# Attention feeding a gated feed-forward layer: q, k and v loaded per head pair and cast on chip, both heads' scores in one two-bank tile, one shared PSUM pool, and the weights loaded behind the third pair

## The chip, the cores and the metric

The kernel runs on one core of one Trainium2 chip. The metric is device time in microseconds (us), the median of several executions. All executions quoted here are of the fast state; the executions of one kernel lie between 0.1% and 1.1% apart (1.1% in e9). A ratio is the mean time of one kernel's fast runs over the mean of the other's of the same rounds, so it is not quite the ratio of the medians quoted.

The names of the engines: PE is TensorE's matmul stream, PEld its weight loads, DVE is VectorE, ACT is ScalarE, POOL is GpSimd, SP is SyncE, which only issues transfers here. "L203" is a line of the kernel's source. In the kernel with the change, and in every variant, POOL's lines are: L166 and L167 cast q and k, L173 scales v, L203 is the causal mask, L283 is `rs`, the last step of the norm. (Line numbers move by a few in some variants; the names say what it is.)

## The reference

```python
# q, k, v: (8 batches, 8 heads, 576, 64) fp32; f: (8, 8, 576), in 0.8 .. 1.0
cum    = cumsum(log(clip(f, 1e-4, 1)))
scores = q @ k^T / 8 + (cum_i - cum_j), masked above the diagonal
attn   = softmax(scores)
x      = (attn @ v), heads joined: 4608 rows of 512
# feed-forward, d_ff = 1536
xn  = x / rms(x) * rms_g
out = (silu(xn @ w_gate) * (xn @ w_val)) @ w_out
```

Both kernels fold the decay into v: exp of the plain scores is masked, and v, with a column of ones beside it, is multiplied by `exp(mid - cum_j)`. The same matmul then gives numerator and denominator.

## The kernel before

Batch 0's attention runs alone; this is the prologue. Then nine groups of 512 rows go through the feed-forward, and the attention of batches 1 to 7 is woven between their matmuls. `LEAD = 6` puts some attention work of batch 1, called the lead below, ahead of the first gate in program order. The last groups have no attention beside them; they are the tail.

The loads. q and k come with a cast to bf16 in the transfer, issued by POOL, a whole batch at a time; v comes from SP in fp32 and is scaled by POOL.

```python
def load_qk(b):
    for j in range(NB):
        p0, n = j * 128, min(128, S - j * 128)
        for src, dst in ((q, qb[b % 2]), (k, kb[b % 2])):
            nc.gpsimd.dma_start(
                out=dst[0:n, j, :].rearrange("p (h d) -> p h d", d=D),
                in_=src[b, :, p0:p0 + n, :].rearrange("h p d -> p h d"))
# ... (cut)
load_qk(0); load_v(0)
# ... (cut: constants)
for i in range(3):
    load_w(i)          # POOL: 512 columns of w_gate and of w_val each
load_qk(1); load_v(1)
load_wo()              # POOL: w_out in two transfers
for _, work in attention(0):
    work()
```

PSUM, the memory that matmuls write, is used as eight banks of 512 fp32 columns. Scores have three tiles of one bank, the feed-forward three, transposes and values one each.

```python
ps_tr = ctx.enter_context(tc.tile_pool(name="ps_tr", bufs=1, space=PSUM))
ps_sc = ctx.enter_context(tc.tile_pool(name="ps_sc", bufs=3, space=PSUM))
ps_o = ctx.enter_context(tc.tile_pool(name="ps_o", bufs=1, space=PSUM))
ps_f = ctx.enter_context(tc.tile_pool(name="ps_f", bufs=3, space=PSUM))
```

Scores go head by head; a head pair's two heads lie in the two halves of the 128 rows.

```python
def scores(b, p, bank):
    for par in range(2):
        # ... (cut)
        rows = slice(par * 64, par * 64 + 64)
        sc = ps_sc.tile([128, 512], F32, name="sc")
        for kj, q0, n, c in BANKS[bank]:
            nc.tensor.matmul(sc[:, c:c + n], lhsT=KT[b, p][rows, kj * 128:(kj + 1) * 128],
                             rhs=QT[b, p][rows, q0:q0 + n], start=True, stop=True)
        t = PT[b, h]
        nc.scalar.activation(t[:, bank * 512:(bank + 1) * 512], sc, ACT.Exp, scale=scale)
        # ... (cut: masks on POOL for banks 0 and 2)
```

The gate uses two tiles of its own:

```python
def gate(g, fc):
    pg = ps_f.tile([128, GT], F32, name="ff")
    # ... four matmuls with wg into pg
    nc.scalar.activation(t, pg, ACT.Tanh, scale=0.5)
    nc.vector.scalar_tensor_tensor(a, in0=t, scalar=1.0, in1=pg, op0=ALU.add, op1=ALU.mult)
    pv = ps_f.tile([128, GT], F32, name="ff")
    # ... four matmuls with wv into pv
    nc.vector.scalar_tensor_tensor(hTs[g][:, fc, :], in0=a, scalar=0.5, in1=pv, op0=ALU.mult, op1=ALU.mult)
```

The softmax here doesn't subtract the row's maximum and nothing guards it: scores larger than these inputs give would overflow.

Of the kernel before, what the change touches and what calls it, by code (L numbers as in the profile page):

```python
# [23 lines left out]
def kernel(  # L24
# [12 lines left out]
    nc = tc.nc  # L37
# [11 lines left out]

    consts = ctx.enter_context(tc.tile_pool(name="consts", bufs=1))  # L50
    ldp = ctx.enter_context(tc.tile_pool(name="ldp", bufs=1))
    vp = ctx.enter_context(tc.tile_pool(name="vp", bufs=6))
    qkt = ctx.enter_context(tc.tile_pool(name="qkt", bufs=2))
    ptp = ctx.enter_context(tc.tile_pool(name="ptp", bufs=5))
# [4 lines left out]
    hp = ctx.enter_context(tc.tile_pool(name="hp", bufs=2))  # L59
    ep = ctx.enter_context(tc.tile_pool(name="ep", bufs=3))  # L60
    ps_tr = ctx.enter_context(tc.tile_pool(name="ps_tr", bufs=1, space=PSUM))
    ps_sc = ctx.enter_context(tc.tile_pool(name="ps_sc", bufs=3, space=PSUM))
    ps_o = ctx.enter_context(tc.tile_pool(name="ps_o", bufs=1, space=PSUM))
    ps_f = ctx.enter_context(tc.tile_pool(name="ps_f", bufs=3, space=PSUM))


    qb = [ldp.tile([128, NB, H * D], BF16, name=f"qb{i}") for i in range(2)]
    kb = [ldp.tile([128, NB, H * D], BF16, name=f"kb{i}") for i in range(2)]
    Vs = [ldp.tile([128, NB, H, D + 1], BF16, name=f"Vs{i}") for i in range(2)]
    PT4 = [[ldp.tile([128, 5 * 64], BF16, name=f"PT4_{i}{j}") for j in range(2)] for i in range(2)]  # L70


    def load_qk(b):
        for j in range(NB):
            p0, n = j * 128, min(128, S - j * 128)
            for src, dst in ((q, qb[b % 2]), (k, kb[b % 2])):
                nc.gpsimd.dma_start(  # L77
                    out=dst[0:n, j, :].rearrange("p (h d) -> p h d", d=D),
                    in_=src[b, :, p0:p0 + n, :].rearrange("h p d -> p h d"))

    v32s = {}

    def load_v(b):
        for j in range(NB):
            p0, n = j * 128, min(128, S - j * 128)
            v32 = v32s[b, j] = vp.tile([128, H, D], F32, name="v32")
            nc.sync.dma_start(out=v32[0:n, :, :],
                              in_=v[b, :, p0:p0 + n, :].rearrange("h p d -> p h d"))

    fr = consts.tile([BH, S], F32)  # L90
    nc.sync.dma_start(out=fr, in_=f.rearrange("b h s -> (b h) s"))

    for t in qb + kb:
        nc.vector.memset(t[64:128, NB - 1, :], 0.0)
    load_qk(0)
    load_v(0)
    for t in Vs:
        nc.vector.memset(t[64:128, NB - 1, :, :], 0.0)
    for pair in PT4:
        for t in pair:  # L100
            nc.vector.memset(t[:, 4 * 64:], 0.0)
# [5 lines left out]

    rg = consts.tile([128, NDC], F32)
    with nc.allow_non_contiguous_dma(reason="512 gains, once"):
        nc.sync.dma_start(out=rg, in_=moe_rms_g.rearrange("(c p) -> p c", p=128))  # L110
    mhalf = consts.tile([128, NB], F32)
    nc.gpsimd.memset(mhalf, -0.5)

# [18 lines left out]
    nc.vector.tensor_scalar(fr, in0=fr, scalar1=1e-4, op0=ALU.max, scalar2=1.0, op1=ALU.min)  # L132
    nc.scalar.activation(fr, fr, ACT.Ln)
# [4 lines left out]
    nc.vector.tensor_tensor_scan(cum, ones, fr, 0.0, ALU.mult, ALU.add)  # L138
# [3 lines left out]
    dec = consts.tile([BH, NB * 128], F32)  # L142
    nc.vector.memset(dec[:, S:], 0.0)
    nc.scalar.activation(dec[:, 0:S], cum, ACT.Exp, scale=-1.0, bias=mid[:, 0:1])
    decT = consts.tile([128, NB, BH], F32)
    for j in range(NB):
        dps = ps_o.tile([128, BH], F32, name="po")
        nc.tensor.transpose(dps, dec[:, j * 128:(j + 1) * 128], ident_f[0:BH, 0:BH])
        nc.vector.tensor_copy(decT[:, j, :], dps)


    QT, KT, PT = {}, {}, {}
    xs, xTs = {}, {}

    def scale_v(b):
        for j in range(NB):
            v32 = v32s.pop((b, j))
            n = min(128, S - j * 128)
            dj = decT[0:n, j, b * H:(b + 1) * H]
            nc.gpsimd.tensor_tensor(Vs[b % 2][0:n, j, :, 0:D], v32[0:n, :, :], bcast(dj, D), ALU.mult)  # L160
            nc.gpsimd.tensor_copy(Vs[b % 2][0:n, j, :, D], dj)

    def transposes(b, p):
        for src, store, nm in ((qb[b % 2], QT, "QT"), (kb[b % 2], KT, "KT")):
            tp = ps_tr.tile([128, NB * 128], BF16, name="tr")
            for j in range(NB):  # L166
                nc.tensor.transpose(tp[:, j * 128:(j + 1) * 128], src[:, j, p * 128:(p + 1) * 128], ident)  # L167
            t = store[b, p] = qkt.tile([128, NB * 128], BF16, name=f"{nm}{p}")
            nc.vector.tensor_copy(t, tp)

    def scores4(b):

        for par in range(2):  # L173
            sc = ps_sc.tile([128, 512], F32, name="sc")
            rows = slice(par * 64, par * 64 + 64)
            for p in range(4):
                nc.tensor.matmul(sc[:, p * 64:(p + 1) * 64], lhsT=KT[b, p][rows, 512:640],
                                 rhs=QT[b, p][rows, 512:576], start=True, stop=True)
            t = PT4[b % 2][par]
            nc.scalar.activation(t[:, 0:256], sc[:, 0:256], ACT.Exp, scale=scale)  # L180
            d = t[:, 0:256].rearrange("p (h q) -> p h q", q=64)
            nc.gpsimd.affine_select(out=d, in_=d, pattern=[[0, 4], [1, 64]], compare_op=ALU.is_ge,
                                    fill=0.0, base=0, channel_multiplier=-1)
# [5 lines left out]
        ((1, 128, 384, 0), (3, 384, 128, 384)),  # L189
        ((0, 512, 64, 0), (1, 512, 64, 64), (2, 512, 64, 128), (3, 512, 64, 192), (2, 256, 256, 256)),  # L190
    )
    COL = {(0, 0): 0, (1, 1): 512, (3, 3): 896, (2, 2): 1280}

    def scores(b, p, bank):
        for par in range(2):
            h = 2 * p + par
            if bank == 0:
                PT[b, h] = ptp.tile([128, 1536], BF16, name="PT")
            rows = slice(par * 64, par * 64 + 64)
            sc = ps_sc.tile([128, 512], F32, name="sc")  # L200
            for kj, q0, n, c in BANKS[bank]:
                nc.tensor.matmul(sc[:, c:c + n], lhsT=KT[b, p][rows, kj * 128:(kj + 1) * 128],  # L202
                                 rhs=QT[b, p][rows, q0:q0 + n], start=True, stop=True)  # L203
            t = PT[b, h]
            nc.scalar.activation(t[:, bank * 512:(bank + 1) * 512], sc, ACT.Exp, scale=scale)  # L205
            if bank == 0:
                d = t[:, 0:128]
                nc.gpsimd.affine_select(out=d, in_=d, pattern=[[1, 128]], compare_op=ALU.is_ge,  # L208
                                        fill=0.0, base=0, channel_multiplier=-1)
            if bank == 2:  # L210
                d = t[:, 512:1408]
                d = bass.AP(tensor=d.tensor, offset=d.offset, ap=[d.ap[0], [384, 3], [1, 128]])
                nc.gpsimd.affine_select(out=d, in_=d, pattern=[[0, 3], [1, 128]], compare_op=ALU.is_ge,  # L213
                                        fill=0.0, base=0, channel_multiplier=-1)
# [165 lines left out]
```

## Time and profile before

485.8 us, median of 3 runs (485.55 to 486.83); the profiled execution spans 484.0 us.

| before | |
|---|---|
| first full feed-forward matmul (the first gate) | 75.9 us |
| `rs` of batches 0, 1, 7 starts at | 70.1, 115.7, 404.5 us |
| `rs` to `rs` in the steady part | 48.03 us |
| feed-forward of one group, 144 matmuls, 216 ns each | 31.1 us |

The times at which POOL computes `rs`, once a batch, are the best ruler in this kernel. They cut the span in three: up to `rs` of batch 1 (prologue), six batches between `rs` 1 and `rs` 7 (steady part), the rest (tail).

The page's busy times, and its slices, each a fortieth of the span with the busy share in tenths:

```profile
PE 423.9 (88%) x3317; PEld 207.6 (43%) x3317; DVE 260.3 (54%) x534; ACT 222.1 (46%) x436; POOL 187.7 (39%) x335
...
PE   0491707999999999999999999999999999999996
...
POOL 8539990665182518252825282513111211000000
PEclk9999999999999999999999999999999999999999
```

TensorE is full from the eighth slice on. In the first seven it is so in one only, and there POOL is busiest. The windows view gives busy time per engine in a stretch (from:to, length, then busy us with the number of instructions, the granted clock, the share of the 16 DMA engines and GB/s):

```profile
36.00:72.00 36.00, 11.36 (x141) 7.94 (x140) 6.17 (x17) 8.97 (x20) 35.55 (x64) 1.00 1.56 186
...
164.00:356.00 192.00, 187.30 (x1586) 91.90 (x1584) 117.92 (x245) 103.98 (x209) 76.49 (x140) 1.00 0.41 55
```

So there are two stages. In 36:72 POOL is busy 35.6 of 36 us and TensorE 11.4: POOL bounds the prologue, with its issues, masks and v scaling. In four steady batches TensorE is busy 187.3 of 192 us: TensorE bounds the rest. The timeline of TensorE shows what the prologue costs (start, duration, engine, line, operation, count; in brackets the idle time before and what ended it):

```profile
46.41 0.29 PE L231 MATMUL po<-Vs_104,PT 128*128 128x65 bf16 x2 [9.19 <-POOL PT L208]
...
72.66 0.29 PE L258 MATMUL tr<-ident,xn 128*128 128x128 bf16 x1 [10.45 <-DVE xn L252]
...
75.89 0.58 PE L296 MATMUL ff<-xT,wg 128*128 128x512 bf16 x1 [0.58 <-DVE xT L265]
```

### The profile page before, as it was taken

How to read it: one execution, taken by the hardware profiler on the slowest of the kernel's cores; microseconds unless marked ns; L12 is line 12 of the kernel's file. 1: busy time of each engine (PE TensorE's matmuls, PEld its weight loads, DVE VectorE, ACT ScalarE, POOL GpSimd, SP SyncE). 2: the span in 40 equal slices, each digit the busy share in tenths (PEclk: the TensorE clock that was granted, in tenths of full speed). 3: DMA queues.
4: the chain of work that ended last, by engine and by line, in shares of the span. 5: the costliest groups of instructions: out<-in, count | busy, mean ns of one | idle time of the engine just before them, and what ended most of it. 6: DMA issues, size and time to landing. Idle time of an engine off the chain costs nothing.

```text
span 484.0 us, 8505 instructions
## 1 busy us (share of the span) xinstructions
PE 423.9 (88%) x3317; PEld 207.6 (43%) x3317; DVE 260.3 (54%) x534; ACT 222.1 (46%) x436; POOL 187.7 (39%) x335
## 2 busy tenths in 40 slices
PE   0491707999999999999999999999999999999996
PEld 0231403454544454445444544454444544444442
DVE  3210326478447844784478457745774577373670
ACT  3060321664465437544754474447444744232321
POOL 8539990665182518252825282513111211000000
PEclk9999999999999999999999999999999999999999
DMA  9999991594190419041903290010001000201102
GB/s 151 175 195 178 191 187 33 36 65 99 65 120 3 100 66 119 3 100 67 120 1 77 70 118 0 1 66 23 3 0 66 23 1 0 88 1 45 43 1 87
DMA packets 123080, 33.73 MB, mean 70 GB/s; under 512 B 113760, under 2 KB 118368, under 8 KB 123040
## 3 DMA queue, kind: packets, MB, share of 16 engines
q0 software_dynamic: 79744, 14.16, 36.6%
q1 hardware_dynamic: 43296, 19.03, 14.9%
q8 instruction: 26, 0.43, 0.4%
q14 instruction: 14, 0.11, 0.1%
HBM read 37.90 MB, written 9.44 MB: 98 GB/s over the span
## 4 chain that ended last, share of the span: by engine, by line
PE 67%; POOL 13%; issue 6%; DMA 6%; ACT 5%; DVE 2%; POOLq 0%; ACTq 0%
PE ff L311 20%; PE ff L296 14%; PE ff L304 13%; PE sc L202 7%; PE po L231 5%; PE tr L167 4%; DMA wv<-in_moe_w_val_dram 3%; PE tr L258 3%; POOL Vs_104 L160 2%; DMA qb_100<-in_q_dram 2%; ACT junk L245 2%; POOL Vs_105 L160 2%; POOL rs L249 2%; ACT PT L205 2%; POOL qb_100 L77 2%
## 5 line engine op out<-in xcount | busy, mean ns | idle before, releaser
L205 ACT ACTIVATE PT<-sc 128x512 bf16<-128x512 f32 x192 | 105.1, 599 | 87.6 <-PE sc L202 73.8
L296 PE MATMUL ff<-xT,wg 128*128 128x512 bf16 x432 | 114.7, 382 | 0.7 <-DVE xT L265 0.6
L304 PE MATMUL ff<-xT,wv 128*128 128x512 bf16 x432 | 114.0, 380 | 0.0
L311 PE MATMUL ff<-wo,hT 128*128 128x512 bf16 x432 | 112.5, 380 | 0.0
L301 DVE SCALAR_TENSOR_TENSOR ga<-th,ff 128x512 f32<-128x512 f32 x108 | 74.2, 687 | 66.9 <-ACT th L299 66.3
L299 ACT ACTIVATE th<-ff 128x512 f32<-128x512 f32 x108 | 64.5, 598 | 82.6 <-PE ff L296 80.9
L306 DVE SCALAR_TENSOR_TENSOR hT<-ga,ff 128x512 bf16<-128x512 f32 x108 | 74.2, 687 | 9.0 <-PE ff L304 0.3
L304 PEld LDWEIGHTS <-wv 128*128 128x128 bf16 x432 | 42.2, 98 | 50.2 <-issue 2.5
L208 POOL TENSOR_SCALAR_AFFINE_SELECT PT<-PT 128x128 bf16<-128x128 bf16 x64 | 19.1, 299 | 97.8 <-ACT PT L205 97.6
L296 PEld LDWEIGHTS <-wg 128*128 128x128 bf16 x432 | 38.6, 98 | 42.0 <-issue 5.6
L314 ACT COPY ores<-ff 128x512 f32<-128x512 f32 x36 | 21.1, 586 | 75.2 <-PE ff L311 74.4
L213 POOL TENSOR_SCALAR_AFFINE_SELECT PT<-PT 128x384 bf16<-128x384 bf16 x64 | 33.0, 528 | 53.2 <-ACT PT L205 53.1
L311 PEld LDWEIGHTS <-hT 128*128 128x128 bf16 x432 | 36.5, 98 | 36.4 <-issue 9.5
L231 PEld LDWEIGHTS <-PT 128*128 128x128 bf16 x896 | 35.7, 102 | 31.2 <-POOL PT L208 9.7
L234 DVE RECIPROCAL rden<-po 128x5 f32<-128x5 f32 x64 | 12.2, 191 | 55.3 <-PE po L231 55.3
L258 PE MATMUL tr<-ident,xn 128*128 128x128 bf16 x160 | 20.6, 229 | 18.3 <-DVE xn L252 18.0
L231 PE MATMUL po<-Vs_104,PT 128*128 128x65 bf16 x448 | 22.7, 206 | 13.6 <-POOL PT L208 9.2
L235 DVE TENSOR_TENSOR x<-po,rden 128x320 f32<-128x320 f32 x64 | 31.4, 490 | 1.7
L245 ACT ACTIVATE junk<-x 128x512 bf16<-128x512 f32 x40 | 25.0, 624 | 9.0 <-DVE x L235 8.4
L258 PEld LDWEIGHTS <-xn 128*128 128x128 bf16 x160 | 12.4, 100 | 37.0 <-DVE xn L252 29.1
L265 DVE TENSOR_SCALAR xT<-tr,rg 128x512 bf16<-128x512 bf16 (+7 forms) x64 | 20.5, 362 | 12.3 <-PE tr L258 12.1
L252 DVE TENSOR_SCALAR xn<-x,rs 128x512 bf16<-128x512 f32 x40 | 18.1, 520 | 13.2 <-POOL rs L249 13.2
(300 smaller groups left out, 387.8 us busy)
## 6 DMA issues: line engine op xcount, KB each, us to landing
out_dram<-ores SPq DMA_DIRECT2D x36, 256.0 KB, 2.0
qb_100<-in_q_dram POOLq DMA_DIRECT2D x16, 128.0 KB, 5.3
kb_102<-in_k_dram POOLq DMA_DIRECT2D x16, 128.0 KB, 5.4
qb_101<-in_q_dram POOLq DMA_DIRECT2D x16, 128.0 KB, 4.4
kb_103<-in_k_dram POOLq DMA_DIRECT2D x16, 128.0 KB, 4.5
wg<-in_moe_w_gate_dram POOLq DMA_DIRECT2D x3, 512.0 KB, 12.7
wv<-in_moe_w_val_dram POOLq DMA_DIRECT2D x3, 512.0 KB, 14.0
wo<-in_moe_w_out_dram POOLq DMA_DIRECT2D x2, 768.0 KB, 12.3
```

Of the source, the lines that this page charges most:

```text
L202: nc.tensor.matmul(sc[:, c:c + n], lhsT=KT[b, p][rows, kj * 128:(kj + 1) * 128], rhs=QT[b, p][rows, q0:q0 + n], start=True, stop=True)
L205: nc.scalar.activation(t[:, bank * 512:(bank + 1) * 512], sc, ACT.Exp, scale=scale)
L213: nc.gpsimd.affine_select(out=d, in_=d, pattern=[[0, 3], [1, 128]], compare_op=ALU.is_ge, fill=0.0, base=0, channel_multiplier=-1)
L231: nc.tensor.matmul(po[:, qi, :], lhsT=weights_of(b, h, qi, kj), rhs=Vs[b % 2][:, kj, h, :], start=(kj == 0), stop=(kj == qi))
L245: nc.scalar.activation(junk, x[:, j, :], ACT.Square, accum_out=sq[:, j:j + 1])
L258: nc.tensor.transpose(tp[:, j * 128:(j + 1) * 128], xn[:, j, dc * 128:(dc + 1) * 128], ident)
L296: nc.tensor.matmul(pg, lhsT=wg[:, dc, fc * 128:(fc + 1) * 128], rhs=xT[:, dc, :], start=(dc == 0), stop=(dc == NDC - 1))
L299: nc.scalar.activation(t, pg, ACT.Tanh, scale=0.5)
L301: nc.vector.scalar_tensor_tensor(a, in0=t, scalar=1.0, in1=pg, op0=ALU.add, op1=ALU.mult)
L304: nc.tensor.matmul(pv, lhsT=wv[:, dc, fc * 128:(fc + 1) * 128], rhs=xT[:, dc, :], start=(dc == 0), stop=(dc == NDC - 1))
L306: nc.vector.scalar_tensor_tensor(hTs[g][:, fc, :], in0=a, scalar=0.5, in1=pv, op0=ALU.mult, op1=ALU.mult)
L311: nc.tensor.matmul(po, lhsT=hTs[g][:, fc, j * 128:(j + 1) * 128], rhs=wo[:, fc, :], start=(fc == 0), stop=(fc == NFC - 1))
```

## The change

The intent has two parts. In the prologue, POOL should no longer issue the loads: SP loads q, k and v of one head pair at a time in fp32, DVE (batch 0) or POOL (later batches) casts them, and attention of batch 0 can follow pair by pair. The weights come later, behind the third pair (pair 2, counting from 0). In the steady part, the two heads' score matmuls alternate between the two row halves of the array into the two banks of one tile, and one exp covers 1024 columns. For that, scores, gates and output products share a pool of three two-bank tiles. The last key block of both heads is one full 128-row matmul against a block-diagonal QB. Smaller edits come with it: DVE shares the squares of batch 0's norm, the transposes of x go between the next batch's scores, and the hidden layer has one tile for each column block.

```diff
+    NP = H // 2
+    NST = 3
-    ps_sc = ctx.enter_context(tc.tile_pool(name="ps_sc", bufs=3, space=PSUM))
-    ps_f = ctx.enter_context(tc.tile_pool(name="ps_f", bufs=3, space=PSUM))
+    ps_b = ctx.enter_context(tc.tile_pool(name="ps_b", bufs=3, space=PSUM))
 ... (cut)
+    def load(n):
+        b, h0 = n // NP, 2 * (n % NP)
+        tq, tv = qk32[n % NST], v32[n % NST]
+        for src, c in ((q, 0), (k, 5)):
+            for h in range(2):
+                nc.sync.dma_start(out=tq[:, c:c + 4, h, :],
+                                  in_=src[b, h0 + h, 0:512, :].rearrange("(j p) d -> p j d", p=128))
 ... (cut: the last 64 rows; v in the same way)
+    def take(b, p):
+        n = b * NP + p
+        t = qkb[b, p] = qbp.tile([128, 9, 2, D], BF16, name="qkb")
+        eng = nc.vector if b == 0 else nc.gpsimd
+        eng.tensor_copy(t[:, 0:5, :, :], qk32[n % NST][:, 0:5, :, :])
+        eng.tensor_copy(t[:, 5:9, :, :], qk32[n % NST][:, 5:9, :, :])
 ... (cut)
+        for rows, j0, j1 in ((128, 0, 4), (64, 4, 5)):
+            dj = decT[0:rows, j0:j1, b * H + h0:b * H + h0 + 2]
+            last = nc.gpsimd.tensor_tensor(Vs[b % 2][0:rows, j0:j1, h0:h0 + 2, 0:D],
+                                           v32[n % NST][0:rows, j0:j1, :, :], bcast(dj, D), ALU.mult)
+        load(n + NST)
+        if n == 2:
+            with tc.issue_after(last.ins):
+                for i in range(3):
+                    load_w(i)
+                load_wo()
 ... (cut)
+    def score(sc, b, p, kj, q0, n, c):
+        for par in range(2):
+            rows = slice(par * 64, par * 64 + 64)
+            nc.tensor.matmul(sc[:, par, c:c + n], lhsT=QK[b, p][rows, KEYS[kj]:KEYS[kj] + 128],
+                             rhs=QK[b, p][rows, q0:q0 + n], start=True, stop=True)
 ... (cut: last key block, masks on POOL, values)
     def gate(g, fc):
-        pg = ps_f.tile([128, GT], F32, name="ff")
+        bg = ps_b.tile([128, 2, GT], F32, name="bg")
+        pg, pv = bg[:, 0, :], bg[:, 1, :]
 ... (the four matmuls into pg)
         nc.scalar.activation(t, pg, ACT.Tanh, scale=0.5)
-        nc.vector.scalar_tensor_tensor(a, in0=t, scalar=1.0, in1=pg, op0=ALU.add, op1=ALU.mult)
-        pv = ps_f.tile([128, GT], F32, name="ff")
+        nc.vector.scalar_tensor_tensor(t, in0=t, scalar=1.0, in1=pg, op0=ALU.add, op1=ALU.mult)
 ... (the four matmuls into pv)
     def project(g, j):
-        po = ps_f.tile([128, DM], F32, name="ff")
+        if j % 2 == 0:
+            outs[g] = ps_b.tile([128, 2, DM], F32, name="bg")
+        po = outs[g][:, j % 2, :]
```

## The prediction

> **What bounds the kernel now.** Two stages.
>
> Prologue: the first full feed-forward matmul starts at 75.9 us (timeline). From 12 to 84 us TensorE is busy only 36.5 of 72 us (windows), while GpSimd (POOL) hardly pauses in 36:72 (35.6 of 36 us). The timeline says why: each casting load of q or k occupies POOL 0.88 us to issue, between them POOL waits 1.3 to 2.1 us for older DMAs, and the masks of the first scores (scored at 22.7 us) come only at 46.1 us; TensorE waits 9.2 us for them. Norm then waits behind POOL's scaling of v.
>
> Steady state: the norms' rs stand 48.03 us apart: one batch of attention and one group of feed-forward (144 matmuls of 512). In the tail 48 such matmuls take 10.38 us, 216 ns each, so a group is 31.1 us and attention costs 16.9 us a batch. Start-to-start distances of TensorE in 164:356 split it: scores 5.7 us, values 3.9, q/k transposes 2.8, x transposes 1.2, waits beside feed-forward matmuls 3.1. TensorE bounds here.
>
> **What the change does.**
> 1. POOL issues only the 8 weight DMAs (0.75 to 0.83 us each, 6 us), after scaling pair 2; q, k, v come from SP. Packets of 256 B landed at up to 807 per us (64:68), so a pair's 3456 take 4.3 us: estimate, pairs land at about 9, 13, 17, 22 us, and attention of batch 0 follows pair by pair. Last pair's scores end at 29, values at 34, norm (squares shared by ACT and DVE, 2.4 instead of 3.7 us) and transposes take 7: first gate at about 41 us instead of 76, saving 35. Weights alone ran at 205 packets per us (24:32), 5 us per 512-column pair, 23 us in all, in time for the gates.
> 2. The two heads' score matmuls use opposite row halves and now alternate, in different banks. The Trainium skill, "TensorEngine Tiling (Array Packing)", Key Properties, says tiles run in parallel, and Gotcha 1 that row tiles write different banks. Before, ten 64-row matmuls (1024 columns) already went in 0.37 us, so part of this exists; full pairing is 12 x 0.22 = 2.6 us a batch against 5.7; I take 3.5. Four transposes fewer save 0.2.
> 3. One exp of 1024 columns: from 599 ns at 512 and 382 at 256, about 1.03 us against 1.20. ACT has room; little gain outside the prologue.
> 4. Added on POOL: casts [...] and QB copies, in place of the issues.
> 5. Shared PSUM: three two-bank tiles, each held longer; I allow 0.3 us more waiting a batch.
>
> Net steady: 48.03 to about 45.8 us, 7 batches, 16 us. Total 485.8 - 35 - 16 = 435 us.
>
> **What would show it.** First gate near 41 us, no long POOL gap before the first values; rs 45.5 to 46.5 us apart; scores about 3.5 us a batch; tail unchanged at 216 ns; exp near 1.03 us.
>
> **What would make it wrong.** TensorE's in-order queue waiting for POOL casts in each pair (4 x 1 to 2 us a batch), PSUM tiles coming free late (project holds one for 5 us), weights late for gates 4 to 11, or POOL blocked by weight issues in the prologue: each gives 5 to 15 us back. Better pairing or a prologue under 37 us would go below 425.
>
> Predicted 435 us, range 423 to 450; faster by over 2%: 0.97, within 2%: 0.02, slower: 0.01.

## More of the kernel before

The longest of TensorE's waits in the steady part is the wait for the norm (waits view of TensorE over 164:356; total us, times, longest):

```profile
PE tr L258 <- DVE xn L252: 3.8, 4, 1.0
PE sc L202 <- ACT PT L205: 0.8, 4, 0.2
```

## The result, and the profile after

492.0 us, median of 4 runs (491.73 to 492.23), beside 486.0 us for the kernel before in the same rounds: ratio 1.012, 95% interval 1.010 to 1.014. The result is correct. The change was predicted to win some 10% and loses 1.2%.

The ruler shows where the 6.5 us of the two spans (490.5 against 484.0) came from:

| from the traces, us | first `rs` | first gate | prologue, to `rs` 1 | steady, `rs` 1 to 7 | tail, from `rs` 7 | span |
|---|---|---|---|---|---|---|
| before | 70.1 | 75.9 | 115.7 | 288.8 | 79.5 | 484.0 |
| after | 69.5 | 87.5 | 117.0 | 291.3 | 82.2 | 490.5 |
| difference | -0.6 | +11.6 | +1.3 | +2.5 | +2.7 | +6.5 |

No part gained anything; only the tail had not been meant to. The first gate comes 11.6 us later although the first `rs` does not: in the changed kernel TensorE does 9.8 us of batch 1's attention (77.6 to 87.4) ahead of it, whereas in the kernel before the first gate stands 5.8 us after `rs`, between the transposes of x. So `rs` 1 is the fairer measure of the prologue. The page of the kernel with the change:

```profile
PE 410.2 (84%) x3317; PEld 203.7 (42%) x3317; DVE 259.7 (53%) x540; ACT 210.1 (43%) x354; POOL 169.9 (35%) x349
...
PE   1641027897999899989998999899989998999996
...
POOL 1592154737552535253535353433242211000000
PEclk9965555999999999999999999999999999999999
```

PE is busy 13.7 us less than before, so the change did take work off TensorE, and yet the span is longer. The gap has moved: TensorE and POOL are both nearly idle in slices four and five.

**The prologue.** Windows of the kernel with the change:

```profile
48.00:60.00 12.00, 0.00 (x0) 0.00 (x0) 0.00 (x0) 0.00 (x0) 1.27 (x2) 0.50 1.20 201
...
164.00:356.00 192.00, 181.88 (x1575) 89.81 (x1574) 115.53 (x243) 95.61 (x164) 77.45 (x162) 1.00 0.33 83
```

For 12 us no engine but POOL does anything, and POOL does 1.3 us. The waits view over 24:90 names three waits of one chain; the last line is where it starts:

```profile
ACT junk L279 <- DVE x L265: 26.9, 1, 26.9
...
PE po L261 <- POOL PT_0_111 L203: 23.0, 1, 23.0
POOL qkb L166 <- DMA qk_2_105<-in_k_dram: 15.9, 1, 15.9
```

The last values matmuls of batch 0 wait for a mask on POOL. POOL's timeline shows why the mask is late:

```profile
25.55 1.00 POOL L126 DMA_DIRECT2D wg<-in_moe_w_gate_dram  x1
...
40.92 1.40 POOL L173 TENSOR_TENSOR Vs_110<-v_1_107,decT 128x512 bf16<-128x512 f32 x2 [2.65 <-DMA v_1_107<-in_v_dram]
58.27 0.72 POOL L166 CAST qkb<-qk_2_105 128x640 bf16<-128x640 f32 x1 [15.95 <-DMA qk_2_105<-in_k_dram]
58.93 0.61 POOL L167 CAST qkb<-qk_2_105 128x512 bf16<-128x512 f32 x1
62.28 1.05 POOL L173 TENSOR_TENSOR Vs_110<-v_2_108,decT 128x512 bf16<-128x512 f32 x1 [2.74 <-DMA v_2_108<-in_v_dram]
63.28 0.29 POOL L203 TENSOR_SCALAR_AFFINE_SELECT PT_0_111<-PT_0_111 128x128 bf16<-128x128 bf16 x1
```

The mask of batch 0, 0.29 us of work, stands in POOL's program order behind the cast of q and k of a pair of batch 1 (`qk_2_105`, the pair that is sixth in order; "pair 5", counting from 0) and behind the scaling of its v. In this trace POOL took its work in that order. It waits for that pair's k until 58.27 us and for its v until 62.28 us; then the mask runs, and TensorE resumes:

```profile
63.63 0.24 PE L261 MATMUL po<-Vs_109,PT_0_111 128*128 128x65 bf16 x1 [22.99 <-POOL PT_0_111 L203]
```

Why was pair 5 so late? The chain of work that ended last, in order of time (start, us, what), runs through SP's issue of that pair's loads:

```profile
26.04 0.61 SPq L96
...
30.32 1.39 SPq L93
31.77 2.97 SPq L93
34.78 3.19 SPq L93
38.02 3.93 SPq L93
41.99 3.62 SPq L96
...
47.13 15.02 DMA v_2_108<-in_v_dram
62.28 1.05 POOL Vs_110 L173
```

An issue of L96 that took SP 0.6 us at 26 us takes it 3.6 us at 42 us, and those of L93 take 3 to 4 us. The packet records show what went on beside it. A packet here is one record of the profile, a single move of 256 B or 1 KB. Counted per 4 us, by the start of the packet:

```
              q, k, v packets (256 B)     weight packets (1 KB)
  20:24              2600                        0
  24:28              2241                       15
  28:32               255                      536
  32:36               559                      626
  36:40               603                      612
  44:48               601                      598
  52:56               588                      618
  60:64              1492                       14
  64:68              2403                        0
```

POOL puts all 4,608 weight packets into its queue between 25.6 and 32.2 us. From then on, until most of the weights are in at about 58 us (the last at 61), the two queues get equal numbers of packets. The loads fall from about 600 packets per us to 150, and since their packets are a quarter of the size, to 38 GB/s (150 x 256 B). The Trainium skill, "DMA: Bandwidth & Descriptors", section "Queues, rings and completion order", says that each engine round-robins between the queues that it has work for, at packet granularity. Its packet is a group of descriptors, so its turn is not the single move counted here, and the records don't show how many moves go in one turn. What this trace shows is that the turns come out equal in number of moves: 603 to 612, 601 to 598. An estimate from the two rates alone agrees: weights by themselves went at 202 per us (24:32 in the kernel before), loads by themselves at 650 (20:24 here); one of each in turn gives 154 of each per us, and 150 were measured.

So the prologue's gap is a product of two things: loads slowed by the weights, and an order on POOL in which batch 0 waits for a load of batch 1. Which of the two matters is a question for experiments.

**The steady part.** TensorE is busy 181.9 of 192 us instead of 187.3. Its waits over 164:356:

```profile
PE tr L295 <- DVE xn L289: 4.3, 4, 1.1
PE bg L199 <- DVE QK L190: 2.3, 4, 0.6
PE bg L346 <- DVE th L344: 1.2, 4, 0.3
PE bg L357 <- DVE hT L348: 0.8, 4, 0.2
```

The views count only long idle spells. I therefore added up all start-to-start distances of TensorE's matmuls between `rs` 2 and `rs` 6, and call "wait" what a distance exceeds the operation's own streaming time (216 ns for 512 columns, 29.5 for 65, 56 for a transpose) by. Single missing matmul records, gaps of 432 ns between feed-forward matmuls, are filled in. Per batch:

| us per batch | before | after |
|---|---|---|
| feed-forward, 144 matmuls | 31.1 | 31.1 |
| scores, streaming | 2.51 | 1.24, and 0.22 for the last block |
| entering the 64-row mode, 96 ns each | 1.63 (17 times) | 1.34 (14 times) |
| from the last score to the next other matmul | 3.43 | 3.24 |
| transposes of q, k and x | 3.36 | 3.14 |
| values | 3.54 | 3.54 |
| waits | 2.45 | 4.73 |
| sum | 48.0 | 48.6 |

Pairing works: paired matmuls start 3 to 4 ns apart, and the streaming of scores halved. But scores were only 7.6 us with all their switches, and came to 6.0. The 1.8 us that were gained with the transposes are outweighed by 2.3 us of new waiting. Where the new waits come from shows when TensorE's and DVE's timelines are put side by side. First TensorE, then DVE:

```profile
242.40 0.60 PE L340 MATMUL bg<-xT,wg 128*128 128x512 bf16 x2
243.08 1.02 PE L346 MATMUL bg<-xT,wv 128*128 128x512 bf16 x4
...
245.74 0.19 PE L261 MATMUL po<-Vs_109,PT 128*128 128x65 bf16 x1
245.94 1.02 PE L346 MATMUL bg<-xT,wv 128*128 128x512 bf16 x4
```

```profile
242.34 0.69 DVE L344 SCALAR_TENSOR_TENSOR th<-th,bg 128x512 f32<-128x512 f32 x1 [0.59 <-ACT th L343]
...
245.20 0.69 DVE L344 SCALAR_TENSOR_TENSOR th<-th,bg 128x512 f32<-128x512 f32 x1 [0.38 <-ACT th L343]
```

Each time the second product of a gate (L346, into bank 1 of its tile) starts 0.05 us after DVE has finished L344 (242.34 + 0.69 = 243.03; 245.20 + 0.69 = 245.89), which only reads bank 0 of that tile. No data passes between them. Before, the two products had tiles of their own and there was no such wait. So what orders them seems to be that both touch one tile; e1 and e10 test it. In the tail the same pattern makes a group take 34.3 us instead of 31.1 (first gate to first gate).

### The profile page after: what moved, and what is told of

It reads as the page before. It is cut to its first block, busy times and chain, and to the rows that moved or that the text cites. A ratio compares the mean times of both kernels' runs of the same rounds, so it can differ in the third digit from the quotient of the medians.

```text
span 490.5 us, 8797 instructions
## 1 busy us (share of the span) xinstructions
PE 410.2 (84%) x3317; PEld 203.7 (42%) x3317; DVE 259.7 (53%) x540; ACT 210.1 (43%) x354; POOL 169.9 (35%) x349
## 3 DMA queue, kind: packets, MB, share of 16 engines
q1 hardware_dynamic: 120464, 37.92, 31.6%
## 4 chain that ended last, share of the span: by engine, by line
PE 62%; ACT 11%; DVE 8%; SPq 5%; DMA 4%; issue 4%; POOL 4%; POOLq 0%; ACTq 0%; DVEq 0%
PE bg L357 19%; PE bg L346 17%; PE bg L340 14%; ACT junk L279 4%; PE po L261 4%; ACT th L343 3%; SPq L93 3%; DMA v_2_108<-in_v_dram 3%; PE tr L188 3%; PE bg L199 3%; DVE xn L289 2%; ACT PT L235 2%; PE tr L295 2%; DVE th L344 2%; POOL rs L283 2%
## 5 line engine op out<-in xcount | busy, mean ns | idle before, releaser
L340 PE MATMUL bg<-xT,wg 128*128 128x512 bf16 x432 | 115.1, 379 | 0.0
L346 PE MATMUL bg<-xT,wv 128*128 128x512 bf16 x432 | 109.3, 378 | 3.4 <-DVE th L344 1.8
L343 ACT ACTIVATE th<-bg 128x512 f32<-128x512 f32 x108 | 64.5, 597 | 109.4 <-PE bg L340 106.1
L235 ACT ACTIVATE PT<-bg 128x1024 bf16<-128x1024 f32 x96 | 97.1, 1023 | 33.2 <-PE bg L199 32.8
L357 PE MATMUL bg<-wo,hT 128*128 128x512 bf16 x432 | 105.8, 379 | 2.1 <-DVE hT L348 1.2
L344 DVE SCALAR_TENSOR_TENSOR th<-th,bg 128x512 f32<-128x512 f32 x108 | 74.0, 686 | 48.3 <-ACT th L343 48.2
L348 DVE SCALAR_TENSOR_TENSOR hT<-th,bg 128x512 bf16<-128x512 f32 x108 | 74.0, 685 | 33.3 <-PE bg L346 33.2
L203 POOL TENSOR_SCALAR_AFFINE_SELECT PT<-PT 128x256 bf16<-128x256 bf16 (+1 forms) x96 | 46.5, 486 | 105.7 <-ACT PT L235 105.3
L346 PEld LDWEIGHTS <-wv 128*128 128x128 bf16 x432 | 40.3, 97 | 50.1 <-issue 13.4
L357 PEld LDWEIGHTS <-hT 128*128 128x128 bf16 x432 | 40.0, 98 | 42.1 <-issue 2.8
L340 PEld LDWEIGHTS <-wg 128*128 128x128 bf16 x432 | 37.9, 98 | 36.3 <-issue 4.6
L199 PE MATMUL bg<-QK 64*128 64x64 bf16 (+3 forms) x576 | 41.4, 252 | 5.8 <-DVE QK L190 5.8
L188 PE MATMUL tr<-ident,qkb 128*128 128x128 bf16 x288 | 29.8, 234 | 2.9 <-DVE QK L190 2.0
```

Of the source, the lines that this page charges most:

```text
L188: nc.tensor.transpose(tp[:, (c - c0) * 128:(c - c0 + 1) * 128], src[:, c, :, :].rearrange("p h d -> p (h d)"), ident)
L199: nc.tensor.matmul(sc[:, par, c:c + n], lhsT=QK[b, p][rows, KEYS[kj]:KEYS[kj] + 128], rhs=QK[b, p][rows, q0:q0 + n], start=True, stop=True)
L203: nc.gpsimd.affine_select(out=d, in_=d, pattern=pattern, compare_op=ALU.is_ge, fill=0.0, base=0, channel_multiplier=-1)
L235: nc.scalar.activation(t, sc, ACT.Exp, scale=scale)
L340: nc.tensor.matmul(pg, lhsT=wg[:, dc, fc * 128:(fc + 1) * 128], rhs=xT[:, dc, :], start=(dc == 0), stop=(dc == NDC - 1))
L344: nc.vector.scalar_tensor_tensor(t, in0=t, scalar=1.0, in1=pg, op0=ALU.add, op1=ALU.mult)
```

## The experiments

The names: e1 to e4, e6, e7 and e8 change one thing in the kernel with the change ("after"); e5 and e9 to e12 build on each other.

| run | median us (before, same rounds) | ratio, 95% interval | first `rs` | first gate | to `rs` 1 | `rs` 1 to 7 | tail |
|---|---|---|---|---|---|---|---|
| before | 486.0 | 1 | 70.1 | 75.9 | 115.7 | 288.8 | 79.5 |
| after | 492.0 (486.0) | 1.012, 1.010-1.014 | 69.5 | 87.5 | 117.0 | 291.3 | 82.2 |
| e1 products first | 483.3 (486.7) | 0.993, 0.990-0.995 | 68.5 | 86.6 | 114.3 | 290.6 | 79.6 |
| e2 few weights | 468.3 (486.7) | 0.962, 0.959-0.966 | 44.7 | 64.1 | 92.4 | 292.4 | 82.0 |
| e3 casts behind norm | 485.2 (486.7) | 0.997, 0.994-1.001 | 48.8 | 80.5 | 110.6 | 291.3 | 82.0 |
| e4 weights behind norm | 479.3 (486.7) | 0.985, 0.982-0.988 | 44.0 | 66.3 | 107.8 | 288.8 | 82.0 |
| e5 three repairs | 473.3 (487.1) | 0.972, 0.970-0.974 | 44.0 | 66.0 | 101.3 | 289.9 | 79.6 |
| e6 heads apart | 492.9 (487.1) | 1.012, 1.010-1.014 | 67.7 | 86.6 | 115.8 | 292.7 | 82.0 |
| e7 last block apart | 494.9 (487.1) | 1.017, 1.014-1.019 | 62.9 | 83.5 | 115.1 | 296.2 | 82.2 |
| e8 large packets | 486.4 (487.1) | 0.999, 0.996-1.002 | 64.5 | 82.8 | 112.9 | 290.3 | 81.9 |
| e9 weights in steps | 466.0 (486.5) | 0.958, 0.954-0.962 | 44.1 | 64.8 | 93.6 | 288.6 | 79.6 |
| e10 one score tile | 458.8 (486.5) | 0.944, 0.941-0.946 | 45.6 | 55.2 | 98.0 | 280.3 | 79.5 |
| e11 two score tiles | 498.7 (486.5) | 1.025, 1.023-1.027 | 44.0 | 52.3 | 97.1 | 301.1 | 101.3 |
| e12 first weights early | 455.6 (487.2) | 0.937, 0.934-0.939 | 46.1 | 51.5 | 93.4 | 278.4 | 79.5 |

The columns from "first `rs`" on are read from the one profiled execution of each kernel, which can lie 2 to 3 us off the median (e9's and e12's were their fastest, e1's its slowest). The first gates of e10 to e12 stand ahead of the lead, as before, those of the others behind it, so compare prologues by `rs` 1. e2 and e8 give a wrong result; all the others are correct.

### e1: both products of a gate before its tanh

```diff
         # four matmuls into pg
-        nc.scalar.activation(t, pg, ACT.Tanh, scale=0.5)
-        nc.vector.scalar_tensor_tensor(t, in0=t, scalar=1.0, in1=pg, op0=ALU.add, op1=ALU.mult)
         # four matmuls into pv
+        nc.scalar.activation(t, pg, ACT.Tanh, scale=0.5)
+        nc.vector.scalar_tensor_tensor(t, in0=t, scalar=1.0, in1=pg, op0=ALU.add, op1=ALU.mult)
```

> The changed kernel with one edit: in a gate both products are issued before the tanh and the first vector operation. Theory (false wait): because both products now share one two-bank tile, the second product waits for the vector operation that reads the first, although it writes another bank. Then the tail's groups fall from 34.3 to about 31.1 us, norms come about 46.5 us apart instead of 48.55, and the total is about 476 us (470 to 482). Rival (three two-bank tiles are too few): tiles are held as long or longer here, so the tail stays near 34 us a group and the total within 3 us of 492.

It ran in 483.3 us, 8.7 us below the change. A group in the tail is back at 31.1 us (first gate to first gate; expectations below have it as 31.3) and the tail at 79.6. So the false wait is real, and in the tail it was the whole loss. But the expected 470 to 482 us were missed, because in the steady part it gave little: `rs` to `rs` is 47.9 us (46.5 was expected), and the waits of a batch are about as large as before the repair (4.4 to 4.6 us by the same count), now behind other releasers: a gate's first product waits for DVE to finish the previous use of the tile (L340 <- hT), and an output product for an exp (L357 <- ACT PT). The wait had moved. That there are only three two-bank tiles for everything, each held for longer when both products come first, would explain it; this run doesn't show it.

### e2: a twelfth of the weights

```diff
-    wg = consts.tile([128, NDC, DF], BF16)     # wv, wo alike
+    wg = consts.tile([128, 512], BF16)
-            nc.tensor.matmul(pg, lhsT=wg[:, dc, fc * 128:(fc + 1) * 128], ...)
+            nc.tensor.matmul(pg, lhsT=wg[:, fc % 4 * 128:fc % 4 * 128 + 128], ...)
```

The same eight issues at the same place, but few packets; the result is wrong.

> The changed kernel with a twelfth of the weights loaded, in as many DMAs, and used for all feed-forward matmuls (wrong result on purpose). The order that comes out has POOL's last mask of batch 0 ahead of the casts of pair 5. Theory (weight packets slow the loads of pairs 4 and 5, and POOL stands behind the cast of pair 5): pair 5 lands before 40 us, rs of batch 0 at about 40 us instead of 69.5, total about 463 us. Rival (POOL blocked by issuing weights, 6.6 us): only some 7 us less in the prologue, rs at about 62, total about 485.

468.3 us. The first `rs` is at 44.7 us instead of 69.5, and `rs` 1 at 92.4 instead of 117.0. That puts what the weights' transfers cost in the prologue at 24 to 25 us at most, and it is not POOL's issuing, which is all still there. The order of the instructions that the compiler made is not quite the same (the mask of batch 0 now stands ahead of the casts of pair 5), so the run doesn't tell the two causes apart. It also shows that the rest of the estimate was low: even without contention the first gate is at 64 us, not 41, with 9.9 us of it (54.3 to 64.1) spent on the lead.

### e3: POOL's work for pairs 5 to 7 behind the first norm

```diff
         def start(p):
-            take(b, p)
+            if b == 1 and p >= 1:
+                with tc.issue_after(rs_ins[0].ins):
+                    take(b, p)
+            else:
+                take(b, p)
             transposes(b, p)
```

> The changed kernel with POOL's work on pairs 5 to 7 queued behind the norm of batch 0; weights as they were. If only the order on POOL matters, rs of batch 0 comes at about 45 us and the first gate near 50, total about 465 us. If the slowed loads matter too, rs comes at 45 us, but pair 5 still lands at 58 us and TensorE, whose queue has pairs 5 and 6 ahead of the first gates, starts gates only at 70 to 75 us: total about 482 us.

The weights stay where they were, only POOL's order changes, and the first `rs` comes 20.8 us earlier:

```profile
42.88 0.29 POOL L203 TENSOR_SCALAR_AFFINE_SELECT PT<-PT 128x128 bf16<-128x128 bf16 x1
...
48.75 1.21 POOL L283 TENSOR_TENSOR rs<-ms,mhalf 128x5 f32<-128x5 f32 x1
57.80 0.72 POOL L166 CAST qkb<-qk 128x640 bf16<-128x640 f32 x1 [7.84 <-DMA qk<-in_k_dram]
...
71.36 1.40 POOL L173 TENSOR_TENSOR Vs<-v,decT 128x512 bf16<-128x512 f32 x2 [4.28 <-DMA v<-in_v_dram]
72.72 0.52 POOL L192 COPY QB<-QK 64x64 bf16<-64x64 bf16 x2
```

So a change of order alone brings the first `rs` forward. But the total gains only 6.8 us, about what the second expectation said: the first gate is at 80.5 us, because TensorE has the lead ahead of it, and pairs 5 to 7 still land late (57.8 us and after). The blocking came back, too: POOL's copy into QB for the lead (72.72) stands behind the scalings of three v's that wait for their loads, and TensorE waits 11.1 us for it. Blocking and slow loads are in series; taking away one leaves the other.

### e4: the weights behind the first norm

```diff
-        if n == 2:                      # in take()
-            with tc.issue_after(last.ins):
-                for i in range(3):
-                    load_w(i)
-                load_wo()
+        if b == 0:                      # in norm(), behind rs
+            with tc.issue_after(last.ins):
+                for i in range(3):
+                    load_w(i)
+                load_wo()
```

> The changed kernel with all eight weight DMAs issued behind the norm of batch 0 instead of behind pair 2. Theory (contention with loads): pairs 3 to 7 land undisturbed, rs of batch 0 at about 39 us, first weights land some 8 us later, first gate at about 52 us, total about 463 us (455 to 472). Rival (weights must come early, since 9.4 MB take over 23 us): gates wait for weights, no gain, total over 480 us.

479.3 us, short of the 455 to 472 expected. The first `rs` is at 44.0, the first gate at 66.3, but `rs` 1 only at 107.8: the same collision again, later. The eight weight transfers now slow the loads of batch 1, POOL waits 8.1 us for a pair's k, and TensorE waits 7.0 us for a mask behind it.

### e5: e4, with e1, and five stages for the loads in place of three

```diff
-    NST = 3
+    NST = 5
```

> Gate products first (as in e1), weights behind the norm of batch 0 (as in e4), and five staging buffers instead of three, so that pairs 7 and 8 are loaded before the weights start. If slowed loads and the false wait are the two causes, the norms of batches 0 and 1 come at about 44 and 88 us, then every 47.9 us, the tail at 31.3 us a group: about 459 us (452 to 467). If the slowed loads were not what made e4 stop at 70 us (rs of batch 1 at 107.8), deeper staging does nothing: about 471 us.

473.3 us: the expected 452 to 467 were missed, and the total lies near the rival's 471. With two more stages `rs` 1 comes at 101.3 instead of 107.8, but POOL still has to wait 5.05 us for the v of a later pair, while the weights pass. Whether that wait is the cause is left to e9.

### e6: pairing taken back, everything else kept

```diff
-        for kj, q0, n, c in BANKS[bank]:
-            score(sc, b, p, kj, q0, n, c)        # both heads alternate
+        for par in range(2):
+            for kj, q0, n, c in BANKS[bank]:
+                score(sc, b, p, kj, q0, n, c, par)
```

> The changed kernel with the score matmuls of the two heads of a bank one head after the other instead of alternating; same tiles, same exp. If alternation is what shortened the scores from 5.7 to 4.5 us a batch, they go back to about 5.7 and the total rises by 8 to 10 us, to about 501. If the remaining cost is the switch between matmuls of 128 and of 64 rows (312 ns against 216 before a score, 319 after a 512-column pair), that part stays as it is here. Rival (alternation is worth nothing, both run in parallel anyway): total within 2 us of 492.

492.9 us, 0.9 us more than the change, and ratios 1.012 and 1.012: the rival's number (within 2 us of 492) came true, and the totals alone don't tell the two kernels apart. `rs` to `rs` is 48.79 instead of 48.55 us. The streaming of scores goes from 1.24 to 2.02 us a batch, but of these 0.78 us only 0.24 show in the time of a batch (the way out of the mode got 0.2 us shorter, waits 0.3). So the alternation that the change was built around is worth 0.24 us a batch in this kernel, about 2 us in all; in the repaired kernels, which wait less, it was not tested. Of the step down from 2.51 us, 0.27 us stay without alternation (2.02, and 0.22 for the last block).

### e7: the last block's scores in a tile of the shared pool

```diff
-        po = heads_out[b, 2 * p] = ps_o.tile([128, 512], F32, name="po")
-        sc = po[:, 384:512].rearrange("p (r q) -> p r q", q=64)
+        s4 = ps_b.tile([128, 2, 512], F32, name="bg")
+        sc = s4[:, 0, 0:128].rearrange("p (r q) -> p r q", q=64)
```

In the change, the last block's scores share the values' only bank, and values wait for its exp. Here they take one of the three shared tiles, and each head's values take the values' bank by themselves.

> The changed kernel with the scores of the last key block in a tile of their own from the shared pool, not in the bank of the values. Theory (this sharing makes the values wait for that exp, and the score for the bank): values fall from 4.8 to about 4.0 us a batch, the block's own matmul from 0.8 to 0.2, total by 6 to 9 us, to about 484. Rival: a further user of the three two-bank tiles gives it all back, total within 3 us of 492.

494.9 us, slower by 2.9 us than the change, and `rs` to `rs` 49.18. The rival's number came true (within 3 us of 492): a fourth use of the shared tiles costs more than the wait for the values' bank did. That the two-bank tiles are what is scarce fits this, but the run shows only the sum. It pointed to splitting the pool.

### e8: load packets four times as large

```diff
-                nc.sync.dma_start(out=tq[:, c:c + 4, h, :],
-                                  in_=src[b, h0 + h, 0:512, :].rearrange("(j p) d -> p j d", p=128))
+                nc.sync.dma_start(out=tq[:, h, c:c + 4, :],
+                                  in_=src[b, h0 + h, 0:512, :].rearrange("(p j) d -> p j d", p=128))
 ... (cut: v in the same way; tiles, casts and scaling follow the new layout)
```

Four neighbouring rows go to one partition, so a packet has 1 KB (the last 64 rows keep packets of 256 B). The rows are then in another order, and the result is wrong.

> The changed kernel with q, k, v laid out so that four rows of a head are one packet of 1 KB instead of four of 256 B (rows land on other partitions, so the result is wrong on purpose); as many bytes and DMAs, weights at the same place, and the cast of pair 5 still ahead of the last masks on POOL. Theory (the engines serve the two queues packet by packet): in the stretch of the weights the loads get about four times the bytes, pair 5 lands by about 40 us, rs of batch 0 comes at about 48, total about 470. Rival (the queues share bytes or HBM bandwidth, or POOL's issuing of weights is the cause): pair 5 still lands near 58 us, rs near 69, total 485 or more.

In 36:56 the engines serve 468 to 505 load packets and 525 to 551 weight packets per 4 us, still about one for one, and the loads move 80 to 99 GB/s instead of 38. Pair 5's k is there at 44.1 us instead of 58.3:

```profile
44.15 0.72 POOL L166 CAST qkb<-qk 128x640 bf16<-128x640 f32 x1 [5.91 <-DMA qk<-in_k_dram]
...
56.87 1.40 POOL L173 TENSOR_TENSOR Vs<-v,decT 128x512 bf16<-128x512 f32 x2 [9.13 <-DMA v<-in_v_dram]
58.23 0.29 POOL L203 TENSOR_SCALAR_AFFINE_SELECT PT<-PT 128x128 bf16<-128x128 bf16 x1
```

So the two queues share by number of packets and not by bytes. Yet the first `rs` gains only 5 us, and the expected total of 470 was missed: POOL waits 9.1 us more for the v of a pair before the mask's turn comes. In-order blocking gives back most of what faster loads gain.

### e9: e5, with the weights in four steps

```diff
+        step = {6: lambda: load_w(1), 7: lambda: load_w(2), 8: load_wo}.get(n)   # in take()
+        if step:
+            with tc.issue_after(last.ins):
+                step()
-                for i in range(3):      # in norm(), batch 0
-                    load_w(i)
-                load_wo()
+                load_w(0)
```

> As e5 (gate products first, five staging buffers), but the weights in four steps: the first column block behind the norm of batch 0, the others behind POOL's work on pairs 6, 7 and 8, so that loads run free between them. If what e5 lost between 44 and 101 us (5.2 us of POOL waiting for v of pair 8 ahead of masks, and slow loads before) is the same contention, rs of batch 1 comes at about 92 us and the total at about 464 us (458 to 469). If it is the latency of the attention itself on a cold TensorE, rs of batch 1 stays at 101 and the total at 473.

466.0 us, within the expected 458 to 469 and 7.3 below e5, nearly all of it in the prologue: `rs` 1 at 93.6 us instead of 101.3. (The "cold TensorE" of the rival is the half rate at which it runs in the prologue; see the point on pairs below.) That is about what few weights (e2) reached, 92.4, with all the weights loaded, though e2 had three stages for the loads and not five. By these two runs the same bytes cost some 24 us in one lump at 26 us and about 1 us in four pieces, put where the loads are ahead.

### e10: e9, with one two-bank score tile and four single banks

```diff
-    ps_b = ctx.enter_context(tc.tile_pool(name="ps_b", bufs=3, space=PSUM))
+    ps_b = ctx.enter_context(tc.tile_pool(name="ps_b", bufs=1, space=PSUM))
+    ps_f = ctx.enter_context(tc.tile_pool(name="ps_f", bufs=4, space=PSUM))
 ... gate(): pg and pv are tiles of ps_f; tanh stands before the second product again
 ... project(): po is a tile of ps_f
```

> As e9, but the gate as it was changed (second product after the vector operation) and PSUM split: one two-bank tile for scores, four single banks for gate products and projections. Theory (the shared two-bank tiles cost the steady state its gain; waits of TensorE are 4.7 us a batch in the changed kernel and 2.5 before): waits fall to about 3 us and norms come about 46.5 us apart, total 8 us under e9. Rival (one score tile waits 1.3 us for its exp each time): norms 48 us or more apart, total at or above e9.

458.8 us. `rs` to `rs` is 46.64 us (46.5 was expected), the six steady batches 280.3 us instead of 288.6, the tail 79.5. Scores have a single tile and don't miss the others. The gate has the order of the change here, with its second product after the vector operation, and a group of the tail takes 31.1 us: with tiles of their own the products don't wait for each other. In the prologue, the first gates come ahead of the lead again, and now wait 5.2 and 2.0 us for the first columns of `wg` and `wv`.

### e11: two score tiles, two single banks

```diff
-    ps_b = ... bufs=1 ...    ps_f = ... bufs=4 ...
+    ps_b = ... bufs=2 ...    ps_f = ... bufs=2 ...
```

> As e10, with two two-bank tiles for scores and two single banks for gates and projections. Theory of sharing: also under e9, but the tail, where a gate waits for its first bank through tanh and vector operation, gets slower: over 33 us a group; norms about 47 us apart, total about e9. If the tail stays at 31 us and the norms at 46.5 us, single banks are not scarce and it beats e10.

498.7 us, the slowest of all: 40 us lost to moving two of eight banks from the feed-forward to the scores. The direction was expected, but not the size ("total about e9"). A group in the tail, where there are no scores at all, takes 39.5 us:

```profile
PE ff L342 <- DVE th L346: 6.2, 11, 0.8
```

With two banks, a gate waits until DVE has emptied the bank of the one before.

### e12: e10, with the first weights behind pair 3

```diff
-        step = {6: lambda: load_w(1), 7: lambda: load_w(2), 8: load_wo}.get(n)
+        step = {3: lambda: load_w(0), 6: lambda: load_w(1), 7: lambda: load_w(2), 8: load_wo}.get(n)
-        if b == 0:                      # in norm(), behind rs
-            with tc.issue_after(last.ins):
-                load_w(0)
```

> The kernel of the one-score-tile run (458.8 us), with one line moved: the first 512 columns of both gate matrices are issued behind the v scaling of pair 3 (near 34 us) instead of behind the first norm (47.8 us). In that run the first gates still wait 5.2 and 2.0 us for these two transfers, the second gate group starting at 62.4 us. Theory (the prologue is bounded by when transfers are put into the queues): these waits go, the first norm stays near 45.6 us, because batch 0 needs no load any more after 34 us, and the total falls by 3 to 7 us, to 452 to 456 us. Rival (the two queues serve packets one for one, so 1024 weight packets of 1 KB hold back the loads of pairs 5 and 6 by some 7 us, and POOL, in order, waits for pair 5 ahead of work of batch 0 or of the gates' lead attention): the first norm or the second one is later by as much as the gates gain, and the total stays within 2 us of 458.8.

455.6 us (452.9 to 457.0), within the expected 452 to 456, and the fastest kernel, 6.3% below the kernel before. The first `rs` stays (46.1), the first gate comes at 51.5 us, the second at 55.2 (62.4 in e10), and `rs` 1 at 93.4. The 1,024 packets of this step do take turns with the loads, but for 6 us only. In its steady part TensorE has one long wait left, that for the norm:

```profile
PE tr L295 <- DVE xn L289: 7.3, 4, 1.8
```

The account of a batch by distances, as above, is then: scores 6.0 us (as in the change), waits 2.9 us (4.73 in the change, 2.45 before), in all 46.7 us.

## Why the prediction was wrong, point by point

**What bounds the kernel: right.** POOL in the prologue, TensorE after it; both repaired kernels (e10, e12) gained in just these two stages.

**"First gate at about 41 us instead of 76, saving 35": this step failed.** The gate came at 87.5 us, and `rs` 1 1.3 us later than before. Four of its assumptions broke.

- "Pairs land at about 9, 13, 17, 22 us, and attention of batch 0 follows pair by pair." The loads did nearly that: in the kernel with the change the four pairs had landed at 8.9, 14.0, 19.7 and 26.0 us, and the first scores came at 12.9 us instead of 22.7. But the attention didn't follow at their pace, even with nothing in the way: in e12 the last values of the four pairs are out at 22.7, 28.1, 35.1 and 42.1 us, the fourth 16.5 us after its loads had landed (25.6). "Values at 34" was 8 us low for that reason, and the way from there to the first gate takes 9.4 us (42.1 to 51.5), not 7. What sets the pace of a pair no run isolates; it isn't the loads. One thing that the sum left out is that TensorE works in the prologue at half its later rate (in e12 values start 54 ns apart there and transposes 107; in the steady part 29 and 56).
- "Weights alone ran at 205 packets per us, 23 us in all, in time for the gates." They were not alone. It asked when the weights would be there, and never what they would do to the loads beside them. The two queues took turns by packet; the loads fell to a quarter of their rate and pair 5 landed at 58 to 62 us. The weights themselves took from 27 to 61 us.
- The sum goes from the transposes of x straight to the gate. In the kernel with the change 9.8 us of the lead came between. That is so, by the table, in every kernel with the shared pool (first gate 17.9 us or more after the first `rs`) and in none with separate pools (5.4 to 9.7 us). Gates that queue for a shared tile behind the lead's scores would explain it; no run isolates it.
- Under "What would make it wrong" the prediction names TensorE waiting for POOL's casts and POOL blocked by its weight issues, at "5 to 15 us back" each. What came was neither: the issues took POOL 6.6 us, and are all there in e2. POOL itself waited, and some 24 us were lost: batch 0's last mask stood behind a cast and a scaling for batch 1 that waited for the slowed loads. e3 (order alone, first `rs` -20.8 us), e4 (weights moved, -25.5 us) and e2 (few weights, -24.9 us) show that either cure removes this block; e3's total of only -6.8 us shows that order alone isn't enough, and e8 that faster loads alone aren't either. It took transfers put in at the right time (e9, e12).

With the prologue repaired, `rs` 1 comes 22.3 us earlier than before (93.4 against 115.7), not 35.

**"Full pairing is 2.6 us a batch against 5.7; I take 3.5": right mechanism, too large a gain.** The pairs do start 3 to 4 ns apart. By the measure that the prediction used, all distances that begin at a score, scores went from 5.9 us (the prediction had 5.7) to 4.5. What stayed is the change of mode, which the estimate left out: 14 exits a batch, 3.24 of the 4.5 us, and, outside that measure, 14 entries, each making the distance from the matmul before it 312 ns instead of 216. The Trainium skill, "TensorEngine Tiling (Array Packing)", Key Properties, says not only that tiles run in parallel, which the prediction quoted, but also that changing the tiling mode drains TensorE; the trace fits this, at 96 ns an entry whatever matmul came before. e6 then shows that the alternation itself was worth 0.24 us a batch.

**"Shared PSUM: I allow 0.3 us more waiting a batch", and "tail unchanged at 216 ns": failed.** Waits went up by 2.3 us a batch and a tail group by 3.2 us. The prediction thought of how long a tile is held; it missed that two products in one tile are ordered by the tile. e1 shows the false wait (tail group 34.3 to 31.1 us), and e10 that it goes as well when the order stays and the products get tiles of their own. e11 shows that two banks are too few for the feed-forward, and e7 that a further use of the shared tiles doesn't pay. With one score tile and four single banks (e10) 48.55 us a batch became 46.64, 0.8 us above the predicted 45.8.

**Exp and transposes: right.** Exp of 1024 columns took 1,023 ns (1.03 us predicted), q and k transposes 0.22 us a batch less (0.2 predicted). The added casts of a pair took POOL 0.72 + 0.61 = 1.33 us.

In sum: of the 51 us predicted, the change as it stood got none; e12, with the same loads (two more stages), casts, pairing and exp, gets 31.6 (487.2 - 455.6). What stays open: the 2 us a batch that TensorE waits for the norm in e12; the pace of a pair in the prologue; and how e10's gain splits between more tiles and separate tiles, since e9 had already moved the tanh.

## What to carry to other kernels

A transfer is a cost for others too: before moving a big load, ask which small-packet loads it will share the engines with, and put it in pieces where those have a lead. An engine that runs in order must not have, ahead of work on the critical path, an operation that waits for a transfer of the next stage. And a tile is a unit of ordering: operands that don't depend on each other deserve tiles of their own, even where one two-bank tile would save an instruction.

## What the Trainium skill lacked or had wrong

- "DMA: Bandwidth & Descriptors", section "Queues, rings and completion order", has the turn by packet, its packet being a group of descriptors, but not what follows for a queue of small moves beside one of large ones. Here moves of 256 B fell from about 600 to 150 per us (38 GB/s) beside moves of 1 KB, and with moves of mostly 1 KB of its own (e8) the queue got 80 to 99 GB/s. The section "Issuing engines are not separate DMA queues" calls the time to issue usually small beside the transfer, and I found no word on how it grows when the queue is held back: SP's issues took 0.5 to 0.6 us before the weights came and up to 3.9 us beside them (for a transfer that landed 18.3 us after its issue began).
- "TensorEngine Tiling (Array Packing)", Key Properties, says that a change of mode drains TensorE, without a figure. Here an entry from 128-row to 64-row mode made the distance 312 instead of 216 ns, so 96 ns, 14 to 17 times a batch. It says for which sizes to tile, not how much of the gain can be lost to waits: here alternating took 0.78 us a batch off the streaming of scores and 0.24 us off the 48.8 us of a batch.
- "PSUM — Partial Sum Buffer", section "PSUM bank collisions raise a hardware error", asks for PSUM to be guarded by bank and quadrant, or simply by bank; I found no word on a two-bank tile that the program orders as one unit. The wait was visible as a start 0.05 us after the end of an operation on the other bank, and cost 3.2 us per tail group (34.3 to 31.1 us in e1).
- "TensorE: Matmul & The Clock Gate", Part 1, warns that the clock's trace events can't be fully trusted. What it lacks is the case of a missing event: in the trace of the kernel before, the first event comes at 79.4 us and the views read 1.00 throughout, but matmuls of 512 columns start 426 to 427 ns apart at 77 to 79 us and 216 ns apart after 79.4 us. In the kernel with the change the events are there and fit: 0.50 from 31.1 to 85.7 us, and the gates after it start 215 to 221 ns apart. The mean clocks of the two profiles, 1.000 and 0.939, can therefore not be compared as they stand (one execution of the changed kernel reads 0.996 at the same time, 491.9 us); the distances are the thing to read.
